# Quarter products in runs of eight, and the second forward stage in runs of 32 half-width products

## The chip, the cores and the metric

One core of one Trainium2 chip runs the whole program. The metric is device time in microseconds (us). TensorE (PE) multiplies, and its weight loads are recorded apart (PEld). VectorE (DVE), ScalarE (ACT) and GpSimd (POOL) do the rest; SyncE (SP) issues every transfer.

## The reference, cut to what matters

Eight sequences of 3136 positions and 256 channels pass through a spectral block and then through a transform, a norm and an MLP. All is fp32.

```python
X = np.fft.rfft(x, axis=1)                       # 3136 points
Yr = Xr @ w_r - Xi @ w_i + b_r
Yi = Xr @ w_i + Xi @ w_r + b_i
Yr, Yi = soft_threshold(Yr, 0.01), soft_threshold(Yi, 0.01)
x = np.fft.irfft(Yr + 1j * Yi, n=3136, axis=1)
mixed = np.real(np.fft.fft(np.fft.fft(x, axis=1), axis=2))
u = x + mixed
un = (u - u.mean(-1)) / np.sqrt(u.var(-1) + 1e-06)
out = u + np.maximum(un @ w_ch1, 0.0) @ w_ch2    # 256 -> 1024 -> 256
```

## The kernel before, in words

A transform of 3136 points is done as 64 by 49. `b` counts sequences, 0 to 7. The stages of a sequence, by the names of their tiles:

- `p1` (tile `g_f1`; the profile leaves numbers out and prints `g_f`): 64-point forward products. The matrix `fwd_f` is 128 by 128 with two 64 by 64 blocks on its diagonal, so `quarters` (line 398) makes four products of 64 rows by 64 columns by 512 instead of two full ones. Each lies in another quarter of the PE array. The results go from two banks through `ev` to DRAM.
- `p2_f2` (`g_f2`, also printed `g_f`): 49-point forward products. Real and imaginary parts make 98 rows. For each quarter `q` of the frequencies, two `af` tiles hold the weights and two `tff` tiles the 100 columns that are streamed. Before, sixteen products of 98 rows by 128 columns fill four banks, one bank (`ui`) at a time. ACT copies a bank to `xx`, rounds it to `Xh` and later `Xsh`; DVE adds `xs`; POOL makes the low parts `Xl`, `Xsl`.
- `p2_w` (`g_w`), `p2_mix` (`g_mix`), `p2_yt` (`g_yt`, transposes), `p2_g2` (`g_g2`): channel weights, the transform over channels, and the inverse second stage.
- `p3_norm` (`g_g1`, printed `g_g`): the inverse 64-point products, again by `quarters` with `inv_f`; DVE adds them to `mt` into `ut` and takes statistics.
- `p3_tr` (`g_ut`), `p3_mlp1` (`h`), `p3_mlp2` (`o`): transposes and the MLP. Each product of these and of `g_w` and `g_g2` is three products of rounded parts (line 175), because high and low parts are kept apart. ACT takes `hh` out of `h`, and DVE takes `hl`.

An fp32 product that isn't split in this way shows as two rows in the trace. PSUM has eight banks: two for `h`, two for `o`, and four (`gtile`) that all other stages share.

The order on every engine is made when the program is built. Each stage is a generator that yields a due time; a heap resumes the earliest, which fixes priorities, and a scheduler then lays the instructions out under a timing model of its own. Engines run their lists in order. `quarters` keeps its four products together: ACT first writes two words of input into the second bank (the "held" copy, line 402), the first product waits for that, and the others follow at high priority. So a run starts only when all of its banks are free.

Of the kernel before, what the change touches and what calls it, by code (L numbers as in the profile page):

```python
# [10 lines left out]
F32 = mybir.dt.float32  # L11
# [129 lines left out]
T1, ASK, BEHIND = (1.32, 0.25), 1.16, 3  # L141
WTIMES = (1.002, 1.003, 1.151, 1.152, 1.36, 1.42, 1.48, 1.54)
MLAG, NRM, TR = 1.874, -1.239, -0.86


@with_exitstack
def spectral_block(ctx: ExitStack, tc: tile.TileContext, x, w_ri, b_ri, w1, w2,
# [13 lines left out]
    def gtile(name):  # L161
        return ps.tile([128, 512], F32, tag="g", bufs=4, name=name)
# [150 lines left out]
    def n2_rows(t, m, n):  # L313

        return t[m:m + n].rearrange("n r c u d -> (r c u) n d")
# [78 lines left out]
        nn = n if n == 1 else 4 * z  # L394
        behind(BEHIND if b == 1 else 7, out=xf[:, :nn * D].rearrange("p (n d) -> p n d", d=D), in_=x_rows(b, m, nn))

    def quarters(banks, mat, movs, late, behind_=None):

        def one(i, j):
# [3 lines left out]
        if behind_ is None:  # L403
            first = one(0, 1)
        else:
            with tc.issue_after(behind_):
                first = one(0, 1)
        tc.add_manual_dep(first.ins, held.ins.name, mybir.DependencyInfo(mybir.DependencyClass.Sync, mybir.DependencyReason.DATA), reason="bank held")
        with tc.high_priority(), tc.issue_after(first.ins):
            one(1, 0)  # L410
            one(0, 0)
            one(1, 1)

    def p1(b):

        if b == 0:
            yield from p1_first()
            return
        for i in (b, b + 1)[:1 + (b % 2 == 0)]:
            if i not in a_dram:  # L420
# [12 lines left out]
        for ci, (m, n) in enumerate(todo):  # L433
            yield T * (t0 + width * ci / len(todo))
            ask(b, ci, todo, slots, pre)
            i = slots[ci][3]
            xf = pre[ci - i][:, i * 1024:i * 1024 + 1024]
            if n == 1:
                g = gtile("g_f1")
                te.matmul(g[:, :D], fwd_f, xf[:, :D], start=True, stop=True)  # L440
                ev = sb.tile([128, 512], F32, tag="ev", bufs=2, name="ev")
                sc.copy(ev[:, :D], g[:, :D])
                for r in range(2):
                    st_eng.dma_start(out=a_dram[b + r](0)[0][m, 0].rearrange("c u d -> (c u) d"), in_=ev[r * 64:r * 64 + 64, :D])
                continue
            banks = [gtile("g_f1") for _ in range(2)]
            quarters(banks, fwd_f, [[xf[64 * r:64 * r + 64, p * 512:p * 512 + 512] for p in range(2)] for r in range(2)], xf[0:1, 0:2])
            for r, g in enumerate(banks):
                tag, bufs = evs[(2 * ci + r) % len(evs)]
                ev = sb.tile([128, 512], F32, tag=tag, bufs=bufs, name="ev")  # L450
                (va.tensor_copy if r and b != 1 else sc.copy)(ev, g)
                st_eng.dma_start(out=n2_rows(a_dram[b](0)[0], m + 2 * r, 2), in_=ev.rearrange("p (n d) -> p n d", d=D))
        done.add(("a", b))

    def clock2(b, q):
# [28 lines left out]
    def p2_f2(b):  # L484


        for q in range(4):
# [11 lines left out]
            for ui in range(4):  # L499
                yield base + STEP * ui * F2W / 4  # L500
                us = slice(ui * 2, ui * 2 + 2)
                lo_x = lo_v if b == 1 and q == 0 else lo_g
                g = gtile("g_f2")
                gf = g[:, :400].rearrange("p (k c s j) -> p k c s j", k=2, c=2, s=2)
                for s in range(2):
                    yield base + STEP * F2W * (ui / 4 + s / 8)
                    for k in range(2):
                        te.matmul(gf[:, k, :, s], afs[s][:, ui * D + k * 128:ui * D + k * 128 + 128],  # L508
                                  tfs[s][:, ui].rearrange("p (c j) -> p c j", c=2), start=True, stop=True)
                gv = g[:, :400].rearrange("p (k c t) -> p k c t", k=2, c=2)  # L510

                def view(t):
                    return t[..., us, :].rearrange("p k c s j -> p k c (s j)" if len(t.shape) == 5 else "p k s j -> p k (s j)")

                if b == 0:
                    xv_ = view(X)
                    sc.copy(xv_, gv)
                    va.tensor_add(view(Xs), xv_[:, :, 0], xv_[:, :, 1])
                    continue
                xs = sb.tile([128, 2, 2 * S], F32, tag="xs", bufs=2, name="xs")  # L520
                xh, xl, xsh, xsl = (view(t) for t in (Xh, Xl, Xsh, Xsl))
                if ui < 3:
# [12 lines left out]
                lo_x(xsl, xs, xsh)

# [214 lines left out]

    def p3_norm(b):

        def finish(m, n, g, mt):

            ut = sb.tile([128, 2, D], F32, tag="ut", bufs=UTB, name="ut")
            va.tensor_add(ut[:, :n], g[:, :n * D].rearrange("p (n d) -> p n d", d=D), mt)
            gi, g0, z = [(i, g0, z) for i, (g0, z) in enumerate(GROUPS[b % 2]) if g0 <= m < g0 + z][0]
            if m == g0:
                scales[b, gi] = sb.tile([128, 4, 1], F32, tag="rs", bufs=4, name="rs")  # L760
# [16 lines left out]
            uts[b, m] = ut  # L777
# [3 lines left out]
        for m, n in [(4 * i, 4) for i in range(6)] + [(NM - 1, 1)] * (b % 2):  # L781
            t0, T3 = clock3(b, m)
            yield t0 + T3 * (NRM - 0.5 * (n == 1))
            yield from after(("b", b), ("m", b))
# [7 lines left out]
            for r in (1, 0):  # L792
                bb, n2 = (b - 1 + r, m) if n == 1 else (b, NM * r + m)
                mpn, mmn = (d[0:NH].rearrange("(a n2) d -> a n2 d", n2=N2) for d in m_dram[bb])
                p = 64 * r
                nc.sync.dma_start(out=mt[p + 32:p + 64, :n][:, ::-1], in_=mmn[:, 49 - n2 - n:49 - n2])
                af_ld.setdefault("mt", nc.sync.dma_start(out=mt[p:p + 32, :n], in_=mpn[:, n2:n2 + n]).ins)
            if n == 1:
                g = gtile("g_g1")
                te.matmul(g[:, :D], inv_f, bfs[0][:, :D], start=True, stop=True)  # L800
                finish(m, 1, g, mt[:, :1])
                continue
            if b == 0 and m == 0:
                yield from after(("w", 1, 0))
            banks = [gtile("g_g1") for _ in range(2)]
            quarters(banks, inv_f, [[bfs[r][64 * p:64 * p + 64] for r in range(2)] for p in range(2)], bfs[0][0:1, 0:2],
                     w_in[1, 0] if b == 0 and m == 0 else None)
            for p, g in enumerate(banks):
                finish(m + 2 * p, 2, g, mt[:, 2 * p:2 * p + 2])

    def p3_tr(b):
        for gi, (g0, z) in enumerate(GROUPS[b % 2]):
# [163 lines left out]
```

## Time and profile before

| | |
|---|---|
| median of 3 runs | 1846.11 us (1846.04 to 1850.49) |
| the profiled execution, its span | 1846.94 us, 1845.2 us |
| PE busy | 1815.1 us, 98% of the span |
| DVE, ACT, POOL busy | 1192.4, 809.4, 549.3 us |
| mean granted TensorE clock | 0.991 of full speed |

A row's busy time on PE is modelled at its end, and products overlap, so the start of a product to the start of the next tells more than its length.

### The profile page before, as it was taken

To read this page: it belongs to the slowest core of one execution; us is meant where nothing else is said; L and a number is where in the kernel's file an instruction comes from. 1 tells how busy PE (TensorE), PEld (TensorE's weight loads), DVE (VectorE), ACT (ScalarE), POOL (GpSimd) and SP (SyncE) were. 2 spreads that over 40 slices of the span, in tenths; PEclk is the share of its full clock that TensorE was granted. 3 is DMA by queue.
4 is the path that set the end of the run, shared out by engine and by line. 5 is a ranking of instruction groups with operands and counts; after the bars stand their busy time and mean duration, and the time that the engine had idled before them with its cause. 6 is when DMAs were issued, how large, how long until landed. Compare 5 with 4: busy or idle time off the path is not lost.

```text
span 1845.2 us, 29399 instructions
## 1 busy us (share of the span) xinstructions
PE 1815.1 (98%) x10082; PEld 1495.5 (81%) x10082; DVE 1192.4 (65%) x2619; ACT 809.4 (44%) x1873; POOL 549.3 (30%) x1021
## 2 busy tenths in 40 slices
PE   8998999999999999999999999999999999999998
PEld 5666788788888888887888888888888898877788
DVE  4766767776666666656666756666667766755543
ACT  2564554454444544444444444444444454432222
POOL 0003433332233332233342233433233343222110
PEclk8899999999999999999999999999999999999999
DMA  8866653544426533355343644335432532243110
GB/s 259 244 188 173 176 173 101 162 155 125 131 93 185 166 109 118 99 178 162 114 124 124 171 149 132 102 125 164 137 122 85 166 97 89 79 127 108 43 35 34
DMA packets 157934, 245.61 MB, mean 133 GB/s; under 512 B 24208, under 2 KB 105176, under 8 KB 157528
## 3 DMA queue, kind: packets, MB, share of 16 engines
q1 hardware_dynamic: 157784, 243.72, 44.0%
q8 instruction: 80, 1.31, 0.3%
q14 instruction: 70, 0.57, 0.1%
HBM read 140.79 MB, written 102.86 MB: 132 GB/s over the span
## 4 chain that ended last, share of the span: by engine, by line
PE 90%; DVE 4%; DMA 3%; ACT 1%; issue 1%; SPq 1%; POOL 0%; DVEq 0%; ACTq 0%
PE o L175 29%; PE h L175 28%; PE g_w L175 10%; PE g_f L508 5%; PE g_g L175 4%; PE g_yt L708 3%; PE g_g L401 2%; PE g_ut L825 2%; PE g_f L401 2%; PE g_mix L645 2%; PE g_w L554 1%; PE g_mix L647 1%; DVE eo L609 1%; DMA raw_w<-in_w 1%; DMA tff<-c_tf 0%
## 5 line engine op out<-in xcount | busy, mean ns | idle before, releaser
L844 DVE SCALAR_TENSOR_TENSOR hl<-h,hh 128x512 fp32r<-128x512 f32 (+2 forms) x416 | 272.9, 657 | 405.9 <-ACT hh L843 400.4
L843 ACT ACTIVATE hh<-h 128x512 fp32r<-128x512 f32 (+2 forms) x416 | 237.7, 572 | 487.6 <-PE h L175 461.1
L175 PE MATMUL o<-hl,w2h 128*128 128x512 f32 (+2 forms) x832 | 331.0, 398 | 3.4 <-DVE hl L844 3.3
L175 PE MATMUL h<-utl,w1h 128*128 128x512 f32 (+2 forms) x832 | 320.3, 385 | 0.0
L175 PE MATMUL h<-uth,w1l 128*128 128x512 f32 (+2 forms) x832 | 317.6, 382 | 0.0
L175 PE MATMUL o<-hh,w2l 128*128 128x512 f32 (+2 forms) x832 | 317.6, 382 | 0.0
L175 PE MATMUL o<-hh,w2h 128*128 128x512 f32 (+2 forms) x832 | 316.4, 380 | 0.0
L175 PE MATMUL h<-uth,w1h 128*128 128x512 f32 (+2 forms) x832 | 316.2, 380 | 0.0
L851 POOL TENSOR_TENSOR total<-uth,utl 128x256 f32<-128x256 f32 x200 | 145.8, 754 | 422.6 <-DMA out_dram<-total 243.5
L175 PEld LDWEIGHTS o<-hl,w2h 128*128 128x128 f32 x832 | 156.7, 188 | 41.8 <-DVE hl L844 6.7
L175 PEld LDWEIGHTS o<-hh,w2l 128*128 128x128 f32 x832 | 156.4, 188 | 31.1 <-issue 3.2
L175 PEld LDWEIGHTS h<-uth,w1l 128*128 128x128 f32 x832 | 156.9, 189 | 28.6 <-issue 0.8
L175 PEld LDWEIGHTS h<-utl,w1h 128*128 128x128 f32 x832 | 156.8, 188 | 27.5 <-issue 2.4
L175 PEld LDWEIGHTS h<-uth,w1h 128*128 128x128 f32 x832 | 157.0, 189 | 26.6 <-issue 1.6
L175 PEld LDWEIGHTS o<-hh,w2h 128*128 128x128 f32 x832 | 157.1, 189 | 19.2 <-issue 0.8
L508 PEld LDWEIGHTS g_f<-tff,af 98*128 98x128 f32 x1024 | 139.2, 195 | 23.6 <-issue 8.0
L508 PE MATMUL g_f<-tff,af 98*128 98x100 f32 x1024 | 145.6, 278 | 4.5 <-DMA af<-aq 1.9
L168 POOL TENSOR_TENSOR Xl<-xx,Xh 128x400 fp32r<-128x400 f32 x81 | 90.8, 1122 | 97.7 <-ACT Xh L525 92.8
L571 POOL TENSOR_TENSOR Y<-y,m 128x400 f32<-128x400 f32 x56 | 64.5, 1152 | 182.8 <-DVE m L570 175.2
L568 DVE SCALAR_TENSOR_TENSOR y<-g_w,small,ks 128x400 f32<-128x400 f32 x128 | 80.3, 628 | 41.8 <-PE g_w L175 27.6
L739 ACT COPY bev<-g_g 98x512 f32<-98x512 f32 x128 | 74.7, 584 | 64.0 <-PE g_g L175 49.6
L165 DVE TENSOR_TENSOR utl<-g_ut,uth 128x512 fp32r<-128x512 f32 (+2 forms) x104 | 67.3, 653 | 40.9 <-ACT uth L826 40.6
(162 smaller groups left out, 3276.8 us busy)
## 6 DMA issues: line engine op xcount, KB each, us to landing
bd<-bev SPq DMA_DIRECT2D x128, 196.0 KB
mt<-md SPq DMA_DIRECT2D x192, 128.0 KB
bf<-bd SPq DMA_DIRECT2D x96, 256.0 KB
out_dram<-total SPq DMA_DIRECT2D x88, 256.0 KB
af<-ad SPq DMA_DIRECT2D x56, 392.0 KB
md<-mq SPq DMA_DIRECT2D x112, 192.0 KB
ad<-ev SPq DMA_DIRECT2D x84, 256.0 KB
xf<-in_x SPq DMA_DIRECT2D x39, 512.0 KB
```

The lines of the kernel that those rows point to most:

```text
L165: va.tensor_sub(out_, full, hi.bitcast(F32))
L168: gp.tensor_sub(out_, full, hi.bitcast(F32))
L175: last = te.matmul(o, l, r, start=start and i == 0, stop=stop and i == 2)
L401: return te.matmul(banks[i][64 * j:64 * j + 64], mat[rows, rows], movs[i][j], start=True, stop=True)
L508: te.matmul(gf[:, k, :, s], afs[s][:, ui * D + k * 128:ui * D + k * 128 + 128], tfs[s][:, ui].rearrange("p (c j) -> p c j", c=2), start=Tr ...
L568: va.scalar_tensor_tensor(y1, gw, bias[:, c, o:o + 1], ks, op0=ALU.add, op1=ALU.add)
L571: (va if b == 0 or o == 0 else gp).tensor_sub(y[:, o, :, c, :], y1, m)
L708: te.transpose(gt[:100, (v * 2 + o) * 128:(v * 2 + o + 1) * 128], y[:, o, place].rearrange("p c j -> p (c j)"), ident)
L739: sc.copy(bev, g[:98])
L843: sc.activation(hh[:, :w], h[:, :w], AF.Relu)
L844: va.scalar_tensor_tensor(hl[:, :w], h[:, :w], 0.0, hh[:, :w].bitcast(F32), op0=ALU.max, op1=ALU.subtract)
L851: gp.tensor_add(total[:, k, cols], uth[:, k, cols].bitcast(F32), utl[:, k, cols].bitcast(F32))
```

## The change

Three edits. `quarters` takes one or two groups: with two, eight products in four banks run together, after three held copies instead of one. `p1` of sequences 2 to 7 and `p3_norm` (but for the first two groups of sequence 0) call it with two groups. From sequence 1 on, `p2_f2` takes four banks at once and makes its sixteen products as 32 of 98 rows by 64 columns, alternately in the left and the right half of the array, behind three held copies; the four `xx` copies stand behind one another. `p1` of sequences 2 to 7 now copies results back into `xf` and stores from there, and `p3_norm` makes its additions (`add`) before the statistics (`finish`).

```diff
+BURST = 0.03
...
-    def quarters(banks, mat, movs, late, behind_=None):
+    def quarters(mat, groups, behind_=None):
...
-        held = sc.copy(banks[1][0:1, 0:2], late)
...
+        held = [sc.copy(banks[i][0:1, 0:2], late) for n, (banks, movs, late) in enumerate(groups) for i in range(2) if n or i]
+        with tc.issue_after(behind_) if behind_ is not None else nullcontext():
+            first = one(*groups[0][:2], 0, 1)
+        for h in held:
+            tc.add_manual_dep(first.ins, h.ins.name, mybir.DependencyInfo(mybir.DependencyClass.Sync, mybir.DependencyReason.DATA), reason="bank held")
         with tc.high_priority(), tc.issue_after(first.ins):
-            one(1, 0)
-            one(0, 0)
-            one(1, 1)
+            for n, (banks, movs, late) in enumerate(groups):
+                if n:
+                    one(banks, movs, 0, 1)
+                one(banks, movs, 1, 0)
+                one(banks, movs, 0, 0)
+                one(banks, movs, 1, 1)
...
+            groups = []
+            for c in range(ci, ci + (1 if b == 1 else 2)):
+                ask(b, c, todo, slots, pre)
...
+            quarters(fwd_f, groups)
+            for c, (banks, movs, late) in enumerate(groups, ci):
+                xf, m = pre[c - slots[c][3]], todo[c][0]
+                for r, g in enumerate(banks):
+                    if b == 1:
+                        tag, bufs = evs[(2 * c + r) % len(evs)]
+                        ev = sb.tile([128, 512], F32, tag=tag, bufs=bufs, name="ev")
+                    else:
+                        ev = xf[:, r * 512:r * 512 + 512]
+                    (va.tensor_copy if r and b != 1 else sc.copy)(ev, g)
...
+            def prod(g, ui, s, k, cols):
                 gf = g[:, :400].rearrange("p (k c s j) -> p k c s j", k=2, c=2, s=2)
...
+                first = ui * D + k * 128
+                return te.matmul(gf[cols, k, :, s], afs[s][:, first + cols.start:first + cols.stop],
+                                 tfs[s][:, ui].rearrange("p (c j) -> p c j", c=2), start=True, stop=True)
...
+            yield base + STEP * BURST
+            banks = [gtile("g_f2") for _ in range(4)]
+            lates = (afs[1][0:1, 0:2], tfs[1][0:1, 0, 0:2], tfs[0][0:1, 0, 0:2])
+            held = [sc.copy(g[0:1, 0:2], late) for g, late in zip(banks[1:], lates)]
+            todo = [(banks[ui], ui, s, k, slice(64 * h, 64 * h + 64)) for ui in range(4) for s in range(2) for k in range(2) for h in range(2)]
+            first = prod(*todo[0])
...
+            with tc.high_priority(), tc.issue_after(first.ins):
+                for args in todo[1:]:
+                    prod(*args)
+            xxs = []
+            for ui, g in enumerate(banks):
+                xx = sb.tile([128, 2, 2, 2 * S], F32, tag=("xx", "ev")[ui // 2], bufs=2, name="xx")
+                sc.copy(xx, gv(g))
+                xxs.append(xx)
...
+                lo_x = lo_v if ui == 3 or b == 1 and q == 0 else lo_g
...
+        pairs = ([[0], [4]] if b == 0 else [[0, 4]]) + [[8, 12], [16, 20]]
...
+            loads = [load(m, n) for m in ms]
...
+            quarters(inv_f, groups, w_in[1, 0] if b == 0 and ms[0] == 0 else None)
...
+            for m, g, mt in parts:
+                add(m, 2, g, mt)
+            for m, g, mt in parts:
+                finish(m, 2)
```

The order on PE of the program before, at the second quarter of sequence 4 (`p2_f2`, first two banks; a number behind a name tells buffers apart, and x2 means two such products):

```order
L708 MATMUL g_yt_8923<-ident_98,Y_8618 100x128 x3
L508 MATMUL g_f2_8955<-tff_8949,af_8947 128x2x50 x2
L508 MATMUL g_f2_8955<-tff_8953,af_8951 128x2x50 x2
L825 MATMUL g_ut_8975<-ident_98,ut_8663 128x128 x2
L825 MATMUL g_ut_8975<-ident_98,ut_8680 128x128 x2
L508 MATMUL g_f2_8992<-tff_8949,af_8947 128x2x50 x2
L175 MATMUL o_8909<-hl_8940,w2h_738 128x512
```

The same place on PE after the change:

```order
L176 MATMUL h_9343<-uth_8737,w1l_263 128x512
L525 MATMUL g_f2_9199<-tff_9187,af_9185 64x2x50 x4
L525 MATMUL g_f2_9199<-tff_9191,af_9189 64x2x50 x4
L525 MATMUL g_f2_9200<-tff_9187,af_9185 64x2x50 x4
L525 MATMUL g_f2_9200<-tff_9191,af_9189 64x2x50 x4
L525 MATMUL g_f2_9201<-tff_9187,af_9185 64x2x50 x4
L525 MATMUL g_f2_9201<-tff_9191,af_9189 64x2x50 x4
L525 MATMUL g_f2_9202<-tff_9187,af_9185 64x2x50 x4
L525 MATMUL g_f2_9202<-tff_9191,af_9189 64x2x50 x4
L867 MATMUL g_ut_9263<-ident_98,ut_8528 128x128 x2
```

Before, the four banks stand apart, between transposes and MLP products; now all 32 products of the quarter follow one another.

The order on ACT of the program before, at the same place, from the copy of the first of these banks on:

```order
L524 COPY xx_8985<-g_f2_8955 128x400
L826 CAST uth_8848<-g_ut_8975 128x512
L525 CAST Xh_8943<-xx_8985 128x4x100
L534 CAST Xsh_8945<-xs_8984 128x2x100
L843 ACTIVATE hh_9008<-h_9001 128x512
L524 COPY xx_9024<-g_f2_8992 128x400
L525 CAST Xh_8943<-xx_9024 128x4x100
L717 CAST yh_9017<-g_yt_9012 100x512
L534 CAST Xsh_8945<-xs_9023 128x2x100
L843 ACTIVATE hh_9047<-h_9040 128x512
```

And after the change, on ACT; five copies and casts of the first two banks stand ahead of these twelve rows, behind the last `hh`:

```order
L553 COPY xx_9242<-g_f2_9201 128x400
L563 CAST Xsh_9183<-xs_9287 128x2x100
L560 CAST Xh_9181<-xx_9242 128x4x100
L553 COPY xx_9244<-g_f2_9202 128x400
L868 CAST uth_9074<-g_ut_9263 128x512
L563 CAST Xsh_9183<-xs_9319 128x2x100
L560 CAST Xh_9181<-xx_9244 128x4x100
L746 CAST yh_9298<-g_yt_9293 100x512
L563 CAST Xsh_9183<-xs_9377 128x2x100
L404 COPY g_g1_9402<-bf_9384 1x2
L768 COPY bev_9340<-g_g2_9333 98x512
L885 ACTIVATE hh_9499<-h_9492 128x512
```

Before, an `hh` of the MLP stands behind every four of the others; now sixteen others stand ahead of it.

The order on PE of the program before, at a run of quarter products in `p3_norm` of the same sequence:

```order
L401 MATMUL g_g1_9562<-bf_9555,inv_f_95 64x512
L401 MATMUL g_g1_9563<-bf_9554,inv_f_95 64x512
L401 MATMUL g_g1_9562<-bf_9554,inv_f_95 64x512
L401 MATMUL g_g1_9563<-bf_9555,inv_f_95 64x512
```

And one after the change:

```order
L176 MATMUL h_9565<-uth_9074,w1l_263 128x512
L403 MATMUL g_g1_9401<-bf_9385,inv_f_95 64x512
L403 MATMUL g_g1_9402<-bf_9384,inv_f_95 64x512
L403 MATMUL g_g1_9401<-bf_9384,inv_f_95 64x512
L403 MATMUL g_g1_9402<-bf_9385,inv_f_95 64x512
L403 MATMUL g_g1_9403<-bf_9394,inv_f_95 64x512
L403 MATMUL g_g1_9404<-bf_9393,inv_f_95 64x512
L403 MATMUL g_g1_9403<-bf_9393,inv_f_95 64x512
L403 MATMUL g_g1_9404<-bf_9394,inv_f_95 64x512
L176 MATMUL h_9603<-utl_9075,w1h_262 128x512
```

Two runs of four have become one of eight. Over the program, the quarter products stand in 86 runs of four and two of eight before, and in 8 runs of four and 41 of eight after; `p2_f2` has 28 runs of 32.

## Rows read from the trace of the kernel before

**Rows 1.** The page: busy time by engine; share of the ending chain by engine.

```profile
PE 1815.1 (98%) x10082; PEld 1495.5 (81%) x10082; DVE 1192.4 (65%) x2619; ACT 809.4 (44%) x1873; POOL 549.3 (30%) x1021
...
PE 90%; DVE 4%; DMA 3%; ACT 1%; issue 1%; SPq 1%; POOL 0%; DVEq 0%; ACTq 0%
```

**Rows 2.** Busy us by engine in one stretch, then granted clock, DMA share, GB/s.

```profile
800.00:900.00 100.00, 100.00 (x559) 81.23 (x557) 68.35 (x149) 43.37 (x101) 29.63 (x56) 1.00 0.50 152
```

**Rows 3.** All waits of PE, 350 to 1650 us: total us, times, longest us.

```profile
PE g_f L401 <- DVE mq L654: 0.4, 2, 0.2
```

**Rows 4.** Timeline of PE around one run of four quarter products: start, length, instruction.

```profile
1002.40 0.39 PE L175 MATMUL h<-uth,w1l 128*128 128x512 f32 x1
1002.72 1.09 PE L401 MATMUL g_f<-xf,fwd_f 64*64 64x512 f32 x8
1003.74 0.50 PE L175 MATMUL o<-hl,w2h 128*128 128x512 f32 x1
1004.08 0.39 PE L175 MATMUL o<-hh,w2h 128*128 128x512 f32 x1
```

**Rows 5.** Timeline of PE's weight loads, the same run.

```profile
1002.72 0.21 PEld L401 LDWEIGHTS g_f<-xf,fwd_f 64*64 64x64 f32 x8 [0.35 <-issue]
```

**Rows 6.** Timeline of PE where two runs of four adjoin.

```profile
805.52 0.39 PE L175 MATMUL h<-uth,w1h 128*128 128x512 f32 x1
805.74 0.39 PE L175 MATMUL h<-uth,w1l 128*128 128x512 f32 x1
806.06 1.09 PE L401 MATMUL g_g<-bf,inv_f 64*64 64x512 f32 x8
806.97 1.04 PE L401 MATMUL g_f<-xf,fwd_f 64*64 64x512 f32 x8
807.94 0.50 PE L175 MATMUL h<-utl,w1h 128*128 128x512 f32 x1
808.28 0.40 PE L175 MATMUL h<-uth,w1h 128*128 128x512 f32 x1
```

**Rows 7.** Timeline of PE around one bank of the second forward stage.

```profile
1007.98 0.39 PE L175 MATMUL o<-hl,w2h 128*128 128x512 f32 x1
1008.21 1.03 PE L508 MATMUL g_f<-tff,af 98*128 98x100 f32 x8
1009.01 0.47 PE L175 MATMUL o<-hh,w2h 128*128 128x512 f32 x1
1009.33 0.39 PE L175 MATMUL o<-hh,w2l 128*128 128x512 f32 x1
```

**Rows 8.** Timeline of PE's weight loads for that bank.

```profile
1007.98 1.09 PEld L508 LDWEIGHTS g_f<-tff,af 98*128 98x128 f32 x8
```

**Rows 9.** Groups by line and shape: count, busy us, mean ns, idle before.

```profile
L844 DVE SCALAR_TENSOR_TENSOR hl<-h,hh 128x512 fp32r<-128x512 f32 x352 | 242.3, 688 | 369.5 <-ACT hh L843 365.0 <-ACT g_g L402 3.4
...
L508 PE MATMUL g_f<-tff,af 98*128 98x100 f32 x1024 | 145.6, 278 | 4.5 <-DMA af<-aq 1.9 <-DMA tff<-c_tf 1.6 <-DVE y L568 0.6
...
L401 PE MATMUL g_g<-bf,inv_f 64*64 64x512 f32 x384 | 52.3, 614 | 1.6 <-DMA bf<-bd 1.6
...
L402 ACT COPY g_g<-bf 1x2 f32<-1x2 f32 x48 | 7.2, 150 | 17.5 <-DMA mt<-md 6.6 <-DMA bf<-bd 6.4 <-DVE utl L165 1.6
```

**Rows 10.** Timeline of PE at the shortest products, `g_mix`.

```profile
999.92 0.28 PE L645 MATMUL g_mix<-cs,eh 128*100 128x256 f32 x1
1000.04 0.22 PE L647 MATMUL g_mix<-cs,el 128*100 128x130 f32 x1
1000.10 0.31 PE L645 MATMUL g_mix<-cs,eh 128*100 128x256 f32 x1
```

**Rows 11.** Timeline of ACT where it has work queued.

```profile
1012.35 0.49 ACT L524 COPY xx<-g_f 128x400 f32<-128x400 f32 x1 [0.60 <-PE g_f L508]
1012.78 0.58 ACT L717 CAST yh<-g_yt 100x512 fp32r<-100x512 f32 x1
1013.27 0.53 ACT L525 CAST Xh<-xx 128x400 fp32r<-128x400 f32 x1
```

More of the change, by code (lines that the diff above doesn't have):

```diff
@@ L432, in p1 @@
                 ask(b, ci, todo, slots, pre)
-        for ci, (m, n) in enumerate(todo):
+        ci = 0
+        while ci < len(todo):
             yield T * (t0 + width * ci / len(todo))
[L435 to L438, printed above, removed]
+            if todo[ci][1] == 1:
+                ask(b, ci, todo, slots, pre)
+                m, xf = todo[ci][0], pre[ci]
                 g = gtile("g_f1")
@@ L440, in p1 @@
                 te.matmul(g[:, :D], fwd_f, xf[:, :D], start=True, stop=True)
[L441 to L442 removed]
+                ev = xf[:, D:2 * D]
+                sc.copy(ev, g[:, :D])
                 for r in range(2):
[L444 removed]
+                    st_eng.dma_start(out=a_dram[b + r](0)[0][m, 0].rearrange("c u d -> (c u) d"), in_=ev[r * 64:r * 64 + 64])
@@ L445, in p1 @@
+                ci += 1
                 continue
[L446 to L452, printed above, removed]
+            groups = []
@@ new lines, in p1 @@
+            for c in range(ci, ci + (1 if b == 1 else 2)):
+                ask(b, c, todo, slots, pre)
+                i = slots[c][3]
+                xf = pre[c - i][:, i * 1024:i * 1024 + 1024]
+                groups.append(([gtile("g_f1") for _ in range(2)],
+                               [[xf[64 * r:64 * r + 64, p * 512:p * 512 + 512] for p in range(2)] for r in range(2)], xf[0:1, 0:2]))
+            quarters(fwd_f, groups)
[8 more added lines that the diff above has]
+                    (va.tensor_copy if r and b != 1 else sc.copy)(ev, g)
+                    st_eng.dma_start(out=n2_rows(a_dram[b](0)[0], m + 2 * r, 2), in_=ev.rearrange("p (n d) -> p n d", d=D))
@@ L453, in p1 @@
+            ci += len(groups)
         done.add(("a", b))
@@ new lines, in p2_f2 @@
+            if b == 0:
+                for ui in range(4):
+                    yield base + STEP * ui * F2W / 4
+                    g = gtile("g_f2")
+                    for s in range(2):
+                        yield base + STEP * F2W * (ui / 4 + s / 8)
+                        for k in range(2):
+                            prod(g, ui, s, k, slice(0, 128))
+                    xv_ = pair(X, ui)
+                    sc.copy(xv_, gv(g))
+                    va.tensor_add(pair(Xs, ui), xv_[:, :, 0], xv_[:, :, 1])
+                continue
@@ new lines, in p2_f2 @@
+            yield base + STEP * BURST
[4 more added lines that the diff above has]
+            first = prod(*todo[0])
+            for h in held:
+                tc.add_manual_dep(first.ins, h.ins.name, mybir.DependencyInfo(mybir.DependencyClass.Sync, mybir.DependencyReason.DATA), reason="bank held")
@@ new lines, in p2_f2 @@
+            with tc.high_priority(), tc.issue_after(first.ins):
[6 more added lines that the diff above has]
+                xxs.append(xx)
+            for ui, xx in enumerate(xxs):
+                yield base + STEP * (BURST + ui * F2W / 4)
+                lo_x = lo_v if ui == 3 or b == 1 and q == 0 else lo_g
+                xs = sb.tile([128, 2, 2 * S], F32, tag="xs", bufs=2, name="xs")
+                xh, xl, xsh, xsl = (pair(t, ui) for t in (Xh, Xl, Xsh, Xsl))
+                sc.copy(xh, xx)
+                lo_x(xl, xx, xh)
+                va.tensor_add(xs, xx[:, :, 0], xx[:, :, 1])
@@ L780, in finish, with load @@
                 st_eng.dma_start(out=rd[:128 * z].rearrange("(p j) -> p j", j=z), in_=rall[:, :z].rearrange("p j o -> p (j o)"))
[L781 to L784, printed above, removed]
+        def load(m, n):
             mt = sb.tile([128, 4, D], F32, tag="mt", bufs=2, name="mt")
@@ L797, in p3_norm @@
                 af_ld.setdefault("mt", nc.sync.dma_start(out=mt[p:p + 32, :n], in_=mpn[:, n2:n2 + n]).ins)
+            return mt, bfs
+        pairs = ([[0], [4]] if b == 0 else [[0, 4]]) + [[8, 12], [16, 20]]
+        for ms in pairs + [[NM - 1]] * (b % 2):
+            n = 1 if ms[0] == NM - 1 else 4
+            t0, T3 = clock3(b, ms[0])
+            yield t0 + T3 * (NRM - 0.5 * (n == 1))
+            yield from after(("b", b), ("m", b))
+            loads = [load(m, n) for m in ms]
             if n == 1:
+                mt, bfs = loads[0]
                 g = gtile("g_g1")
                 te.matmul(g[:, :D], inv_f, bfs[0][:, :D], start=True, stop=True)
-                finish(m, 1, g, mt[:, :1])
+                add(ms[0], 1, g, mt[:, :1])
+                finish(ms[0], 1)
                 continue
-            if b == 0 and m == 0:
+            if b == 0 and ms[0] == 0:
                 yield from after(("w", 1, 0))
[L805 to L809, printed above, removed]
+            groups = [([gtile("g_g1") for _ in range(2)], [[bfs[r][64 * p:64 * p + 64] for r in range(2)] for p in range(2)], bfs[0][0:1, 0:2])
+                      for mt, bfs in loads]
+            quarters(inv_f, groups, w_in[1, 0] if b == 0 and ms[0] == 0 else None)
+            parts = [(m + 2 * p, g, mt[:, 2 * p:2 * p + 2]) for m, (mt, bfs), (banks, movs, late) in zip(ms, loads, groups) for p, g in enumerate(banks)]
+            for m, g, mt in parts:
+                add(m, 2, g, mt)
+            for m, g, mt in parts:
+                finish(m, 2)
     def p3_tr(b):
```

50 lines of the change are left out of this document (9 added, 41 removed).

## The prediction

> **What bounds the kernel now.** I read the busy times first. PE is busy for 98% of the span, and 90% of the chain that ended last is PE's own work [rows 1]. Such a share could hide a clock or a stage that differs, so next come the stretches: from 800 to 900 us PE is busy throughout at full granted clock, DVE for 68% and ACT for 43%, and the transfers take half of the DMA engines [rows 2]. Third, PE's waits: in the 1300 us from 350 to 1650 it waits 0.4 us in all for anything that the profile names [rows 3]. So through most of the program the time is the sum of what PE's instructions take up, and a microsecond saved there is one saved in the end, as long as the others keep up.
>
> Since a busy PE is not PE at its peak, the cost of a piece must be read from starts. An MLP product starts 0.22 to 0.23 us after the one ahead of it [rows 6]. A run of four quarter products lies between the start at 1002.40 and the start at 1004.08, 1.68 us, in which two MLP products have their place too (0.45 us): the run takes 1.23 us [rows 4]. Where two runs adjoin, the same reckoning from 805.74 to 808.28 gives 2.54 - 0.45 = 2.09 us [rows 6]. So a second run behind a first adds 0.86 us, and 1.23 - 0.86 = 0.37 us is paid once for going into the small tiles and coming out again. In the timeline it is the late start at 1002.72 and the lengthened MLP product at 1003.74 [rows 4].
>
> **Edit 1, runs of eight.** The two orders count 88 runs of quarter products before and 49 after: 39 times 0.37 us are gone, **-14.4 us**. The products themselves stay. This price needs no new behaviour: the trace holds two adjoining runs already.
>
> **Edit 2, half-width products.** A bank of the second stage takes 1009.33 - 1007.98 - 0.45 = 0.90 us now, 0.112 us for each of its eight rows (a product has two) [rows 7]. The groups' count, 1024 rows, is 128 for each sequence [rows 9]; seven sequences change, 896 rows or 112 banks, so 100.8 us. Streaming doesn't need that: the added run of 0.86 us has two halves of 512 columns, 0.43 us each, with four tiles at work at once, which is 0.084 us for 100 columns. The 0.028 us between is the weight load of 128 columns, which is longer than the product that it lies beside. With 64 columns the load is half as long and no longer sets the pace, provided that the two halves of the array load and stream side by side.
>
> The trace before has no product of 128 rows by 64 columns. The nearest rows are the quarter products: two of the four lie in the same rows of the array and different columns, and four stream in the time of one. So I take 0.086 us a step (0.084, and a little for starts), 32 steps for the 32 products' 64 rows, and 0.37 us of going in and out: 2.75 + 0.37 = 3.12 us a run, 87.4 us for 28 runs, **-13.4 us**. The bound below is 0.084 us a step, -15.1 us. The bounds above are rivals 2 to 4.
>
> **What must hide.** Held copies rise from 90 to 215. At 0.15 us each [rows 9] the 125 new ones are 19 us of ACT, which has half its time free [rows 2]. Their price is not their length but their place: ACT stops at one until the bank and the input are there, with the MLP's `hh` behind it, and PE stops behind `hh` and `hl`. I worked the place in the order shown, sequence 4. Bank 0 is full some 0.9 us after the run starts. Seventeen ACT instructions follow up to the end of the next `hh`, started at most 0.49 us apart [rows 11], about 7.8 us; then `hl`, 0.69 us [rows 9]: ready at 9.4 us. PE by then has 3.12 us of the run, 24 MLP products (5.4 us), and 22 short products at 0.06 to 0.12 us [rows 10]: it asks at 9.8 to 11.1 us. It spares 0.4 to 1.7 us, so PE runs on, but the cover is thinner than elsewhere. In `p3_norm` four additions now stand on DVE, two of them ahead of an `hl`; PE has six MLP products and more between. For places that miss by a little I add **+2 us** over the program, an estimate between nothing and the 0.5 us at every run of rival 1.
>
> The in-place copies in `p1` make the next load of `xf` wait for a store, behind which later transfers stand in SP's queue. Eight sequences share 1845.2 us, some 230 us each, so three runs a sequence leave over 50 us for it, with the DMA engines half idle [rows 2]: nothing. The `im` copy becomes a full `xx`, on ACT and off PE's path: nothing, by the same 0.4 us and more.
>
> **Sum.** -14.4 - 13.4 + 2 = -25.8 us. Against the profiled execution, 1846.94 us (its span is 1845.2), that is 1821.1; the median of the runs lies 0.8 us below it, so I say **1820 us**.
>
> **The skill against the trace.** A run's price first: 0.90 us for eight loads and products of one bank is less than load plus stream in turn, and the loads are recorded alongside the products [rows 7, 8]. So a load overlaps a product in the same rows of the array. The Trainium skill's page "TensorE: Matmul & The Clock Gate", in "Part 3: Packing small matmuls", says that weight loads overlap running products only where the row group differs. By that rule the two halves, which share all rows, would load and stream in turn; it is rival 4. The Trainium skill's page "TensorEngine Tiling (Array Packing)", "Key Properties", says that a change of tiling mode drains TensorE; the 0.37 us agree with it.
>
> **Rivals.**
> 1. *The four banks make PE wait* (the slower side). 69 runs, 41 and 28, now need all of the shared banks, and the sixteen ACT instructions ahead of `hh` empty them. For it: the spare 0.4 us. Against: PE's 0.4 us of waits so far. It decides from 27.8 / 69 = 0.40 us a run; at 0.5 us each it costs 34.5 us, 1853 us. Below that it only eats the gain: 0.1 to 0.3 us a run end at 1826 to 1840.
> 2. *The halves load their weights one after the other.* A step then stays at 0.112 us, a run takes 3.95 us, 28 take 110.7, +9.9 us: 1842 us with edit 1. Against it: eight loads of the quarter run end within 0.21 us of the first's start [rows 5].
> 3. *PE can't hand out instructions fast enough.* The shortest pair of load and product before is 0.06 us [rows 10]. 64 such are 3.84 us, 4.21 a run, +17.1 us: 1849 us. Against: eight products of the quarter run start in a burst, but that is too short to show a lasting rate.
> 4. *Loads and streams of the halves in turn*: 0.086 + 0.056 (half of 0.112) a step, 4.91 a run, +36.7 us: 1868 us. Against: rows 7 and 8 as above.
>
> **How the numbers follow.** The forecast, 1812 to 1830, gets 0.68; rival 1 in full 0.09 and in part 0.08; rival 2, 0.07; rival 3, 0.05; rival 4, 0.03. The likeliest range has below it the bound of 0.084 us, no new waits and up to 3 us of waits lost in the first 350 us, where the order changes too; and above it 10 us of new waits. Leaving out rivals 3 and 4 and rival 1 in full, 0.17, the range is 1811 to 1843 us. Within 0.3%, about what a measurement of this kernel tells from no change, lies 1840.6 to 1851.6: rival 2 mostly and rival 3 half, and the upper edge of rival 1 in part, 0.10. Slower: rivals 1, 4 and the rest of 3, 0.13. Faster: 0.77.
>
> **What would show it.** Right: 28 pieces of 64 half-width products, each some 3.1 us from MLP product to MLP product; runs of eight at 2.1 us; PE's waits from 350 us on below some 5 us. Wrong: a piece of 3.9 us or more (rivals 2 to 4), told apart by the start to start of two products in the same half, 0.112, 0.12 or 0.142 us; or PE waiting behind `hl` or the held copies right after the runs (rival 1). The clock should stay at full; if it falls, this reckoning falls too.

## The result and the profile after

The changed kernel takes 1865.82 us (median of 4 runs, 1864.53 to 1868.52) against 1847.26 for the kernel before (1846.04 to 1850.49): a ratio of 1.0098, with a 95% interval of 1.0085 to 1.0112. It is slower by 1%; 1820 us was forecast.

The page of the changed kernel, the lines of [rows 1]:

```profile
PE 1797.9 (96%) x10978; PEld 1478.2 (79%) x10978; DVE 1246.3 (67%) x2646; ACT 824.9 (44%) x1998; POOL 559.0 (30%) x994
...
PE 80%; DVE 9%; DMA 5%; ACT 2%; issue 1%; POOL 1%; SPq 1%; DVEq 0%; POOLq 0%; ACTq 0%
```

PE is busy for 17 us less in a span that is 19 us longer. Its share of the ending chain fell from 90 to 80%, and DVE's and DMA's rose: the work was saved, and waits came in.

That the work was saved can be read at single runs. PE's timeline in the changed kernel (start, length, instruction) at a run of 32 half-width products:

```profile
814.70 0.39 PE L176 MATMUL h<-uth,w1l 128*128 128x512 f32 x1
815.02 2.97 PE L525 MATMUL g_f<-tff,af 98*64 98x100 f32 x64
817.92 0.66 PE L867 MATMUL g_ut<-ident,ut 128*128 128x128 f32 x4
```

It takes 817.92 - 814.70 - 0.23 = 2.99 us, and the transposes behind it are drawn out by up to 0.1 us: 3.0 to 3.1 us, where four banks by [rows 7] took 3.60. The same view at a run of eight quarter products:

```profile
803.97 0.39 PE L176 MATMUL h<-uth,w1l 128*128 128x512 f32 x1
804.28 1.95 PE L403 MATMUL g_f<-xf,fwd_f 64*64 64x512 f32 x16
...
806.50 0.40 PE L176 MATMUL o<-hh,w2h 128*128 128x512 f32 x1
```

It takes 806.50 - 803.97 - 0.45 = 2.08 us, where two runs of four apart took 2.46 by [rows 4].

Now PE's waits in the changed kernel (total us, times, longest us), first the four largest from 120 to 350 us:

```profile
PE g_g L403 <- DMA bf<-bd: 10.7, 1, 10.7
PE g_f L403 <- issue: 4.5, 1, 4.5
PE g_g L176 <- DVE yl L166: 3.4, 1, 3.4
PE h L176 <- DVE hl L886: 2.6, 2, 1.5
```

All rows of that stretch add up to 33.5 us, against 13.5 before. The three largest from 350 to 1650 us, the answer to [rows 3]:

```profile
PE o L176 <- DVE hl L886: 4.5, 11, 1.2
PE o L176 <- DVE rb L917: 3.4, 4, 1.1
PE g_w L176 <- DVE ut L786: 2.5, 1, 2.5
```

In all there are 11.5 us in this stretch, where there were 0.4. The largest wait of all is the 10.7 us for `bf`, and its chain can be followed. PE's timeline around it:

```profile
142.68 0.34 PE L176 MATMUL g_w<-Xsl,wrh 128*128 128x400 f32 x1
142.86 0.35 PE L176 MATMUL g_w<-Xsh,wrl 128*128 128x400 f32 x1
153.96 1.98 PE L403 MATMUL g_g<-bf,inv_f 64*64 64x512 f32 x8 [10.75 <-DMA bf<-bd]
...
156.37 0.54 PE L176 MATMUL g_w<-Xsl,wrh 128*128 128x400 f32 x1
156.70 0.54 PE L176 MATMUL g_w<-Xsh,wrl 128*128 128x400 f32 x1
```

ACT's timeline ahead of it, behind a run of the second forward stage of sequence 1:

```profile
133.18 0.49 ACT L553 COPY xx<-g_f 128x400 f32<-128x400 f32 x1 [1.01 <-PE g_f L525]
...
137.72 0.35 ACT L563 CAST Xsh<-xs 128x200 fp32r<-128x200 f32 x1
137.98 0.58 ACT L768 COPY bev<-g_g 98x512 f32<-98x512 f32 x1
```

SP's timeline of DMA issues in the same stretch:

```profile
133.58 1.41 SPq L770 DMA_DIRECT2D bd<-bev  x2
137.75 0.68 SPq L825 DMA_DIRECT2D mt<-md  x1
...
143.45 0.32 SPq L770 DMA_DIRECT2D bd<-bev  x1
...
148.12 0.33 SPq L494 DMA_DIRECT2D tff<-c_tf  x1
149.86 1.93 SPq L820 DMA_DIRECT2D bf<-bd  x4
```

The run has put twelve copies and casts (133.18 to 137.72) ahead of the last `bev` of sequence 0. Its store to `bd` now stands behind ten loads on SP and is issued at 143.45, and the loads of `bf`, which need it, stand behind one more `tff` and start at 149.86. In the kernel before, ACT's timeline has that copy between the copies and casts of single banks:

```profile
135.41 0.58 ACT L739 COPY bev<-g_g 98x512 f32<-98x512 f32 x1
```

SP's timeline before has that store as the last of three, and `bf` soon behind it:

```profile
136.01 2.83 SPq L741 DMA_DIRECT2D bd<-bev  x3
...
142.81 1.03 SPq L791 DMA_DIRECT2D bf<-bd  x2
```

In the changed kernel PE waits until 153.96; before, the longest wait for `bf` was 1.6 us. The copy to `bev` itself is only 2.6 us later (137.98 against 135.41), the first loads of `bf` 7 us (149.86 against 142.81): its place in SP's queue, and what SP waits for ahead of it, makes the rest. The wait costs twice. Ahead of it the `g_w` products start 0.18 us apart, behind it 0.33: the clock has gone to its lower level, 1.2 GHz. Two windows of 10 us of the changed kernel, busy time by engine and, third from the end, the granted clock:

```profile
140.00:150.00 10.00, 3.21 (x12) 2.87 (x10) 2.97 (x6) 0.49 (x1) 0.10 (x1) 0.67 0.84 249
150.00:160.00 10.00, 6.04 (x22) 4.32 (x23) 3.70 (x11) 1.86 (x4) 0.19 (x1) 0.53 0.64 196
```

Before, the two stand at 0.83 and 1.00. Over 120 to 350 us the granted clock is 0.91 after and 0.98 before; from 0 to 120 us it is the other way round, 0.97 after and 0.91 before.

### The profile page after: what moved, and what is told of

It reads as the page before. It is cut to its first block, busy times and chain, and to the rows that moved or that the text cites. A ratio compares the mean times of both kernels' runs of the same rounds, so it can differ in the third digit from the quotient of the medians.

```text
span 1864.5 us, 31304 instructions
## 1 busy us (share of the span) xinstructions
PE 1797.9 (96%) x10978; PEld 1478.2 (79%) x10978; DVE 1246.3 (67%) x2646; ACT 824.9 (44%) x1998; POOL 559.0 (30%) x994
## 4 chain that ended last, share of the span: by engine, by line
PE 80%; DVE 9%; DMA 5%; ACT 2%; issue 1%; POOL 1%; SPq 1%; DVEq 0%; POOLq 0%; ACTq 0%
PE o L176 26%; PE h L176 25%; PE g_w L176 9%; PE g_f L525 4%; PE g_g L176 4%; PE g_yt L737 2%; PE g_ut L867 2%; PE g_f L403 2%; PE g_g L403 2%; PE g_mix L674 1%; DVE eo L638 1%; DVE hl L886 1%; DMA raw_w<-in_w 1%; PE g_w L583 1%; DVE ut L786 1%
## 5 line engine op out<-in xcount | busy, mean ns | idle before, releaser
L893 POOL TENSOR_TENSOR total<-uth,utl 128x256 f32<-128x256 f32 x200 | 152.2, 785 | 451.3 <-DMA out_dram<-total 210.8
L562 DVE TENSOR_TENSOR xs<-xx 128x200 f32<-128x200 f32 x112 | 89.7, 802 | 35.8 <-ACT xx L553 20.3
L525 PEld LDWEIGHTS g_f<-tff,af 98*64 98x64 f32 (+1 forms) x1920 | 94.5, 142 | 18.6 <-issue 7.2
L525 PE MATMUL g_f<-tff,af 98*64 98x100 f32 (+1 forms) x1920 | 101.3, 254 | 6.2 <-DMA af<-aq 2.1
```

The costliest lines, as they stand in the source:

```text
L525: return te.matmul(gf[cols, k, :, s], afs[s][:, first + cols.start:first + cols.stop], tfs[s][:, ui].rearrange("p (c j) -> p c j", c=2), s ...
L893: gp.tensor_add(total[:, k, cols], uth[:, k, cols].bitcast(F32), utl[:, k, cols].bitcast(F32))
```

## The experiments

Theory A: runs that need all four shared banks at once, and the list of ACT and DVE work that such a run leaves behind it, make TensorE wait, most of all where little other work covers it. Theory B: the runs of eight in `p3_norm` take all four `bf`, both `mt` and all four `ut`, so that nothing can be loaded or added ahead. Theory C came later: the waits only move, whichever sequences change.

The kernels are the changed one with constants put in, shown here with the values that give the change (a single group of `p3_norm` takes additions and statistics bank by bank, as before):

```diff
+P1_PAIR, P3_PAIR, P3_TO = 2, 0, 8
+F2_FROM, F2_TO, F2_BANKS, F2_HALVES = 1, 8, 4, 2
...
-            for c in range(ci, ci + (1 if b == 1 else 2)):
+            for c in range(ci, ci + (1 if b < P1_PAIR else 2)):
...
+        if not P3_PAIR <= b < P3_TO:
+            pairs = [[4 * i] for i in range(6)]
...
+            if not F2_FROM <= b < F2_TO:
+                for ui in range(4):
```

Results together. The shifts are read from starts: by how much the 289th and the 1585th product into `h`, and the last product of all, start later than before (402.5, 1323.9 and 1840.1 us there), in the one execution profiled. The last column sums PE's waits from 350 to 1350 us (0.4 before).

| kernel | median us | ratio to before, 95% | shift at 402, 1324, end | waits |
|---|---|---|---|---|
| the change | 1865.82 | 1.0098 [1.0085, 1.0112] | +20.2, +11.6, +19.5 | 7.9 |
| e1 quarters only | 1843.14 | 0.9991 [0.9977, 1.0005] | +4.1, -6.3, -1.4 | 1.8 |
| e2 second stage only | 1856.29 | 1.0057 [1.0038, 1.0077] | +1.4, +3.8, +7.7 | 7.8 |
| e3 p3_norm in fours | 1860.68 | 1.0079 [1.0055, 1.0104] | +9.0, +11.0, +14.9 | 9.5 |
| e6 sequences 0, 1 as before | 1845.41 | 1.0000 [0.9986, 1.0015] | -1.0, -7.5, +2.2 | 5.9 |
| e7 change in 2 to 6 alone | 1839.93 | 0.9974 [0.9962, 0.9987] | -5.9, -11.4, -8.3 | 7.0 |
| e8 e7 without second stage | 1842.85 | 0.9989 [0.9973, 1.0006] | +4.2, -4.1, 0.0 | 2.4 |
| e4 e7 in full width | 1851.74 | 1.0040 [1.0026, 1.0054] | +1.9, +2.0, +6.3 | 5.0 |
| e5 e7 in runs of two banks | 1847.93 | 1.0018 [1.0003, 1.0033] | -7.7, -7.5, -3.4 | 8.2 |
| e9 second stage from 2 on | 1851.31 | 1.0045 [1.0028, 1.0061] | +5.2, -3.3, +4.1 | 6.9 |
| e10 e7 without held copies | 1854.80 | 1.0063 [1.0046, 1.0081] | +6.3, +6.6, +11.2 | 7.8 |
| e11 e7, two xx on DVE | 1838.34 | 0.9966 [0.9953, 0.9979] | +1.1, -7.8, -4.4 | 5.7 |
| e12 e7, p1 pairs from 3 | 1835.53 | 0.9959 [0.9944, 0.9974] | -8.9, -15.3, -12.3 | 6.4 |
| e13 e12, two xx on DVE | 1835.40 | 0.9956 [0.9944, 0.9969] | -7.1, -15.8, -12.5 | 5.3 |
| e14 e12 without second stage | 1835.63 | 0.9955 [0.9941, 0.9968] | -0.5, -8.7, -4.7 | 1.4 |

The first shift has to be read with care, because it holds what the clock gave in that one execution. In e4, e5, e7, e8, e10 and e11 the first 1389 products on PE stand in the same order, up to about 290 us. The 1389th starts at 287.4 us in e5 and at 296.1 in e11, the earliest and the latest of the six. Busy time by engine and, third from the end, the granted clock, from 0 to 290 us, in e5:

```profile
0.00:290.00 290.00, 266.00 (x1425) 199.20 (x1425) 193.84 (x430) 141.79 (x333) 52.52 (x102) 0.97 0.66 197
```

and in e11:

```profile
0.00:290.00 290.00, 264.44 (x1355) 199.83 (x1356) 188.57 (x413) 139.24 (x324) 50.30 (x95) 0.94 0.66 196
```

0.03 of 290 us is 8.7 us, the whole difference. So a shift at 402 us is not a property of the kernel alone, while between two of these shifts (402 to 1324 us, 1324 us to the end) little of it is left: the granted clock is 1.00 from 402 to 1324 us in every trace. Nor does the traced execution always stand at the median: it took 1842.1 us in e14, 1842.7 in e11 and 1843.4 in e5.

**Each edit alone, and the early part as before.**

```diff
-F2_FROM = 1          # e1
+F2_FROM = 9
-P1_PAIR, P3_PAIR = 2, 0          # e2
+P1_PAIR, P3_PAIR = 9, 9
-P3_PAIR = 0          # e3
+P3_PAIR = 9
-P3_PAIR, F2_FROM = 0, 1          # e6
+P3_PAIR, F2_FROM = 2, 2
```

> The changed kernel, but the second forward stage as before: full-width products, bank by bank. By its starts a run of eight saves 0.37 us, 14.4 us over 39, so without any wait 1846 - 14 = 1832 us. Theory A (runs that need all four shared banks make TensorE wait, the second forward stage's worst of all): most of the 20 us lost by 300 us and of the waits at hl go, 1832 to 1840. Theory B (the runs of eight of p3_norm use all four bf, both mt and all four ut, so that nothing can be loaded or added ahead): the 10.7 us wait at the first p3_norm run and the waits for ut stay, 1850 to 1858.

> The changed kernel, but all quarter products in runs of four (p1 of sequences 2 to 7 still stores from xf). A run of 32 half-width products was 3.03 us in the changed kernel against 3.60 for four banks: 16 us over 28, so without any wait 1830 us. Theory A (four banks at once make TensorE wait): the loss of the first 300 us stays in good part, 1845 to 1855. Theory B (the p3_norm runs of eight are what waits): 1830 to 1838.

> The changed kernel with only p3_norm back in runs of four, addition and statistics of a bank one after the other. 23 runs of eight are undone, 23 x 0.37 = 8.5 us dearer. Theory B: the waits for bf and ut go (10.7 us at 143 us and some 8 us of ut), so 1866 - 19 + 8.5 = 1855 or better. Theory A: nothing but the dearer runs, 1870 to 1875.

> The changed kernel, but p3_norm of sequences 0 and 1 in runs of four and the second forward stage of sequence 1 bank by bank, so that the first 300 us stand nearly as before. Undone are 5 pairs of quarter runs and 4 runs of 32: 1.9 + 2.3 us dearer. If the loss is one of the start (transfers of sequences 0 and 1 behind one another on SP), the 20 us by 300 us go: 1866 - 20 + 4 = 1850 us; what is left above 1822 is then waits of the steady part. If the loss is spread over all sequences: 1860 or more.

e1 lies 3 us above A's range and 7 below B's. e2 is above A's range and far above B's: half-width runs alone (`p1` still stores from `xf`) make the kernel slower. e3 lies between the two theories: it won 5 us (3.5 by the ratios) although its runs are 8.5 us dearer, so the runs in `p3_norm` do lose time too, but the wait for `bf` at 143 us stayed (11.4 us). e6 won 20 us (18 by the ratios): most of the loss stood in sequences 0 and 1.

**Where the early loss sits.** The second stage of sequence 1 alone put back, and p1 of sequence 2 (in the kernel with the change in 2 to 6):

```diff
-F2_FROM = 1          # e9
+F2_FROM = 2
-P1_PAIR, P3_PAIR, P3_TO, F2_FROM, F2_TO = 2, 0, 8, 1, 8          # e12
+P1_PAIR, P3_PAIR, P3_TO, F2_FROM, F2_TO = 3, 2, 7, 2, 7
```

> The changed kernel in all but one thing: the second forward stage of sequence 1 is bank by bank in full width, four runs of 32 fewer. In the kernels with runs of 32 in sequence 1 TensorE waited 10.7, 11.2 and 11.4 us for bf at about 143 us, in those without it 3.2 and 2.7 us. If these four runs set the early loss, the wait at 143 us is 3 us and the time some 13 us lower with what the lower clock took: 1866 - 13 + 2 = 1855 us or less. If the runs of eight in p3_norm of sequence 0 are its cause, the wait stays and the time is above 1862.

> The kernel with the change in sequences 2 to 6, with p1 of sequence 2 in runs of four again (3 runs of eight undone, 1.1 us dearer). At its first run of eight, at 210 us, TensorE waited 2.4 us with the array handing out nothing (4.5 and 5.5 us in the kernels with the whole change there), and the clock fell behind it. If the larger run is the cause, 1840 - 3 = 1837 us; if the transfers of the start are, 1841.

In e9 four runs of 32 less are worth 14.5 us by the medians and 10 by the ratios, and the first rows of PE's waits from 130 to 160 us no longer name `bf`:

```profile
PE g_w L182 <- ACT Xsh L587: 1.8, 1, 1.8
PE g_yt L791 <- POOL Y L654: 1.6, 1, 1.6
PE g_g L409 <- ACT ks L646: 1.5, 1, 1.5
```

So these four runs bring the wait for `bf`. Which link of the chain counts, ACT's copies or the place in SP's queue, no run tells apart.

e12's median is 4.4 us below e7's; by the ratios it is 2.8 us, and the two intervals overlap. In the changed kernel the wait there (4.5 us, "issue") is a run of eight behind a run of eight. The held copies of the second stand on ACT until DVE's additions free the banks of the first, two of which come late, at 229.62. DVE's timeline in the changed kernel:

```profile
226.44 1.28 DVE L786 TENSOR_TENSOR ut<-g_g,mt 128x512 f32<-128x512 f32 x2
...
229.62 1.29 DVE L786 TENSOR_TENSOR ut<-g_g,mt 128x512 f32<-128x512 f32 x2
```

ACT's timeline there, the held copies:

```profile
230.34 0.15 ACT L404 COPY g_f<-xf 1x2 f32<-1x2 f32 x1 [0.42 <-DVE ut L786]
...
231.00 0.15 ACT L404 COPY g_f<-xf 1x2 f32<-1x2 f32 x1
```

In e7 the wait there is 2.4 us, and behind it the clock did not fall: the granted clock from 210 to 230 us is 1.00 in e7, as in e5. In e4, e8, e10 and e11, with the same order on PE up to there and a wait of 2.0 to 2.4 us, it is 0.74 to 0.83. In e12, e13 and e14 the wait is 1.0 us and the clock 1.00. So the run of eight there costs the clock in some executions only, and how much of the 4.4 us is e12's edit is not shown.

**The middle alone; width, banks, and no second stage.**

```diff
-P3_PAIR, P3_TO, F2_FROM, F2_TO = 0, 8, 1, 8          # e7
+P3_PAIR, P3_TO, F2_FROM, F2_TO = 2, 7, 2, 7
-F2_FROM, F2_TO = 2, 7          # e8, against e7
+F2_FROM, F2_TO = 9, 8
-F2_HALVES = 2          # e4, against e7
+F2_HALVES = 1
-F2_BANKS = 4          # e5, against e7
+F2_BANKS = 2
```

> The changed kernel, but p3_norm in runs of eight and the second forward stage in runs of 32 in sequences 2 to 6 alone; sequences 0, 1 and 7 as before. Against the kernel before, the one with sequences 0 and 1 as before stood at -1.0 us at 402 us, gained 6.5 us up to 1324 us and lost 9.7 us from there to the end, with waits for ut at 1467 and 1655 us. Theory A (both ends have too little other work to cover the waits of the larger runs): the loss behind 1324 us goes, some 1837 us. Theory C (waits move to wherever the order is thin, whichever sequences change): 1842 to 1848.

> As the one with sequences 2 to 6 alone, but with the second forward stage bank by bank in full width everywhere: runs of eight alone. In the steady part the quarter runs alone gained 10.4 us from 402 to 1324 us at 1.8 us of waits, while the whole change gained 8.6 there. Theory A: with both ends as before 1847 - 10 to 12 = 1835 us, better than or as good as with the half-width runs. If the half-width runs keep a net gain in the middle, this one is slower than the one with both.

> As the one with sequences 2 to 6 alone, but the four banks are filled by 16 products of 128 columns, still in one run. Tells the width from the gathering of four banks. If the weight load of 128 columns sets the pace (0.112 us a row), a run takes 3.60 us in place of 3.03 and 20 runs are 11 us dearer than in half width, with the same waits behind them. If gathering is what made the run short, it stays at 3.0 to 3.1 us and the time is the same as in half width.

> As the one with sequences 2 to 6 alone, but the half-width products in runs of two banks. By (3.03 - 0.37)/2 + 0.37 a run takes 1.70 us against 1.80 for two full-width banks: over 40 runs 4 us are saved, 7 us less than by four banks. Theory A (it is the need for all four banks that makes TensorE wait): the some 6 us of waits at hl and rb between 350 and 1350 us go, so about as fast as with four banks, 1835 to 1838. If the waits stay, the ACT work behind a run is the cause and not the number of banks: 1842 or more.

e7 (`p1` of sequence 7 keeps its runs of eight) beats both kernels, and lies between A's 1837 and C's 1842 us. Of the 9.7 us that e6 lost behind 1324 us, 3.1 are left, so A holds for the end as for the start, and C has little left. e8 is slower than e7, but its first 402 us are 10 us behind, which is mostly the clock as above; behind 402 us it gains 4.2 us on the kernel before and e7 2.4, so the half-width runs seem to be worth nothing there. e4's median agrees with the forecast of 11 us to 0.8, in part by luck: in the traced executions 6.8 us of its loss on e7 stand behind 402 us, and 7.8 ahead, where the clock differs. What confirms the width is the single run. PE's timeline in e4:

```profile
801.22 0.39 PE L182 MATMUL h<-uth,w1l 128*128 128x512 f32 x1
801.45 3.71 PE L531 MATMUL g_f<-tff,af 98*128 98x100 f32 x32
804.94 0.48 PE L182 MATMUL o<-hl,w2h 128*128 128x512 f32 x1
805.26 0.60 PE L925 MATMUL g_ut<-ident,ut 128*128 128x128 f32 x4
```

805.26 - 801.22 - 0.45 = 3.59 us: gathering alone saves nothing, the width saves 0.5 to 0.6 us a run. e5 missed A's forecast and came out by the other: it is 8 us slower than e7 and its waits (8.2 us) are not fewer, so the number of banks is not by itself what makes PE wait.

**What makes PE wait behind a run.** Both are e7 with one line changed:

```diff
-                halves(banks, 0, list(zip(banks[1:], lates)))          # e10
+                halves(banks, 0, [])
-                    sc.copy(xx, gv(g))          # e11
+                    (va.tensor_copy if ui % 2 else sc.copy)(xx, gv(g))
```

> The kernel with the change in sequences 2 to 6, without the 60 held copies of the second forward stage, so that ACT doesn't stop for a bank and a run begins when its first bank is free. If it is these copies, with hh behind them, that make TensorE wait for hl and rb (7.0 us from 350 to 1350 us), the waits fall below 4 us and the time to some 1836. If it is the sixteen other ACT instructions or DVE, the waits stay, and products of a run are drawn apart: 1840 or more.

> The kernel with the change in sequences 2 to 6, with two of the four copies to xx on DVE. They are 0.49 us each on ACT: 1 us less ahead of the next hh at each of 20 runs. If ACT's queue behind the run is what makes hl late, waits fall by some 3 us and the time to 1836 or 1837. If DVE is (the waits at hl and rb both end with DVE work), they rise: 1841 to 1846.

In e10 the waits stay, and most runs fall apart. PE's timeline, the two pieces of one run:

```profile
801.13 2.28 PE L531 MATMUL g_f<-tff,af 98*64 98x100 f32 x48
803.35 0.50 PE L182 MATMUL o<-hl,w2h 128*128 128x512 f32 x1
...
804.15 0.39 PE L182 MATMUL h<-utl,w1h 128*128 128x512 f32 x1
804.47 0.91 PE L531 MATMUL g_f<-tff,af 98*64 98x100 f32 x16
805.31 0.66 PE L925 MATMUL g_ut<-ident,ut 128*128 128x128 f32 x4
```

The last bank alone takes 805.31 - 804.15 - 0.23 = 0.93 us, no less than 0.90 in full width: half width pays only in long runs, and the held copies are what keeps them long. e10 is also 12 us behind e7 at 402 us. It is 5 us behind already at the 1389th product, ahead of every run that differs, with the clock at 0.74 from 210 to 230 us where e7 has 1.00. The other 7 are not settled. e11 agrees with ACT's queue, weakly: 1.3 us fewer waits; its 1.6 us of time are within the noise.

**What the half-width runs are worth in the end.** e13 is e12 with e11's line, e14 is e12 with F2_FROM = 9:

> The fastest kernel so far (change in sequences 2 to 6, p1 in runs of eight from sequence 3), with two of the four xx copies on DVE. In the kernel with p1 in runs of eight from sequence 2 this took the stretch from 402 to 1324 us from a gain of 5.5 to one of 8.9 us. If ACT's queue behind the runs is what makes hl late, the same 2 to 3 us come here: 1832 to 1834. If that was the order of the moment, 1836 or more.

> The fastest kernel so far without its 20 half-width runs: the second forward stage bank by bank in full width. By starts the runs save 20 x 0.57 = 11 us, if TensorE then waited no more than without them. If the waits behind them take it all back, this kernel is as fast, 1834 to 1838, and its stretch from 402 to 1324 us gains 8 us or more. If part of it stays, this one is slower: 1840 to 1845.

All three take the same time. PE's waits from 350 to 1350 us in e14:

```profile
PE g_w L182 <- POOL Xsl L175: 1.0, 2, 0.7
PE o L182 <- DVE hl L944: 0.4, 1, 0.4
```

The same view of e12:

```profile
PE o L182 <- DVE hl L944: 3.2, 7, 0.9
PE o L182 <- DVE rb L975: 2.0, 3, 1.1
PE o L182 <- DVE mq L737: 0.8, 3, 0.3
PE g_g L409 <- ACT bev L822: 0.4, 2, 0.2
```

From 402 to 1324 us e14 gains 8.2 us on the kernel before, e12 6.4 and e13 8.7. So 17 half-width runs in that stretch, each 0.5 to 0.6 us shorter on PE, are worth nothing: their 9 us are given back, in e12 2 more, 5.0 of them (6.4 - 1.4) in waits that the profile names. The others are not in one place; by starts, the products into `h` and `o` take 4.9 us more in e12 than in e14, the way into and out of the runs included. e13's copies on DVE lower the waits by 1 us, and the time is the same: whether ACT or DVE is the slower one behind a run is not settled.

## Why the prediction was wrong

**The bound** held: through the middle PE's work still sets the time, and whatever it saved without a wait came out (quarter runs alone gained 8.2 to 10.4 us from 402 to 1324 us in e14 and e1).

**Edit 1, -14.4 us:** right in size. A run of eight takes 2.08 us where 2.09 was reckoned.

**Edit 2, -13.4 us:** right in size. A run takes 3.0 to 3.1 us where 3.12 was reckoned, and e4 confirms that the width makes it, not the gathering. That it is the load of 128 columns that sets 0.112 us a row fits, but no run tells it from other effects of the width. Rivals 2, 3 and 4 (3.95, 4.21 and 4.91 a run) fell with that. Rival 4's rule, in "Part 3: Packing small matmuls" of the Trainium skill's page "TensorE: Matmul & The Clock Gate", isn't borne out by the trace: 32 loads and products in the same rows would have taken 4.91 us in turn, and took 3.0 to 3.1.

**What must hide, +2 us: this step failed.** "I worked the place in the order shown, sequence 4", found 0.4 to 1.7 us to spare, and added 2 us for the whole program, with "up to 3 us of waits lost in the first 350 us" in the range. PE's waits over the whole span rose from 25.1 to 61.3 us (the sums of all rows): +36 us where +2 was added. Of these, 2.7 came up to 120 us, 20.0 from there to 350 us, 7.5 from 350 to 1350 us and 6.0 behind that. Put against the 27.8 us saved, that is +8 us; the span grew by 19.3. For the other 11 us the lower clock is part of the account: one minus the granted clock, over the first 350 us, comes to 15.4 us before and 24.3 after (from 0.91 and 0.98, 0.97 and 0.91). This is 9 us more at most, since some of it fell into the waits themselves; no run separates the amount. Where the loss sat is shown by taking parts back one after the other: the second stage of sequence 1 (1.0098 to 1.0045, e9), `p3_norm` of sequences 0 and 1 (to 1.0000, e6), `p3_norm` and the second stage of sequence 7 (to 0.9974, e7), p1 of sequence 2 (to 0.9959, e12). These are 30 us by the medians and 26 by the ratios, the last step not clear of noise, and the runs undone were themselves worth some 8 (eight of 32 products at 0.5 to 0.6, eleven of eight at 0.37). A place in the middle of the program was taken for all of them. Why the start is worse is read from the timelines: PE has less other work there (before, it was busy for 216.5 of the 230 us from 120 on, and for 999.6 of the 1000 us behind), stores and loads of two sequences share SP's queue, and a copy that stands 2.6 us later behind twelve ACT instructions ends as a wait that is 9 us longer.

**Rival 1** named the mechanism, waits behind runs that need four banks, and missed its place: in the middle it is the "part" case (7.9 us from 350 to 1350 us), which just eats what edit 2 gains; the full price is paid in sequences 0, 1 and 7, and perhaps in `p1` of 2. Its tie to the number of banks is not confirmed (e5).

**xf stored in place, "nothing":** not tried by itself. e12 keeps the store, so what it won on e7 isn't the store's. **The clock** "should stay at full": it fell to 0.91 from 120 to 350 us, and the prediction had said that its reckoning falls with it.

The chance given to the slower side, 0.13, and the upper end, 1843 us, were too small for a term worked out at one place of some seventy.

## What to carry to other kernels

Price a saving on the busiest engine where it stands, but check its cover at the ends of the program first, where nothing else fills a wait: here the runs of eight gained in sequences 2 to 6, the half-width runs gained nothing there, and putting `p3_norm` and the second stage back in 0, 1 and 7 took the ratio from 1.0098 to 0.9974. Gathering short instructions into one long run saves their entry price and gathers their followers too: read what the next engine's list and the DMA queue then hold ahead of the next thing that is waited for. A change that applies to every iteration can be taken for the middle ones alone; that version (e12) beats both kernels, at 0.9959 [0.9944, 0.9974], and so does it without the half-width runs (e14). And before a shift between two single executions is given a cause, compare their granted clocks up to that point.

## What the runs showed of the hardware

- Two halves of the array that share all 98 rows load and stream side by side: 32 products of 64 columns in 3.0 to 3.1 us, 16 of 128 columns in 3.59. A single bank in half width takes 0.93 us against 0.90, so what is paid once a run takes back what one bank saves.
- With one wait of 10.7 us the granted clock went to 0.67 and 0.53 in two slices of 10 us; in e9, without this wait, it was 0.95 and 0.90 there. Products behind the wait started 0.33 us apart in place of 0.18.
- The same order on PE can take 287.4 or 296.1 us to the same product, at granted clocks of 0.97 and 0.94 (e5, e11). The shifts at 402 us, from -8.9 in e12 to +6.3 in e10, hold such differences: the granted clock from 0 to 402 us is 0.98 in e12 and 0.96 in e10, 8 of the 15 us between them.
